# Windowed attention and a channel mix on one core: two phases over DRAM become one loop of 12 units kept on chip

## The chip, the cores and the metric

The kernel runs on one core of a Trainium2 chip. The metric is the time of one execution on the device in microseconds (us), taken as the median of several runs. One execution was also recorded by the hardware profiler; what is read from the profile and the trace is that execution. TensorE (PE) multiplies matrices, with its weight loads shown as PEld, VectorE is DVE, ScalarE is ACT, GpSimd is POOL, and SyncE (SP) issues DMAs.

## The reference

Inputs q, k, v are float32 of 4 batches x 8 heads x 768 tokens x 64. Each query sees the first 4 keys (the sinks) and the last 128 keys up to its own. The heads, side by side, are the 512 channels of x, which goes through a channel mix with a hidden width of 1024.

```python
scores = scale * np.matmul(q, k.transpose(0, 1, 3, 2))
keep = is_sink | in_window            # pos < 4, or 0 <= rel < 128
a = softmax(where(keep, scores, -1e9))
x = np.matmul(a, v)                   # heads side by side: (4, 768, 512)
x_prev = x shifted by one token, zero in front
xk = mu_k * x + (1.0 - mu_k) * x_prev
xr = mu_r * x + (1.0 - mu_r) * x_prev
k = np.maximum(xk @ w_k, 0.0)
v = k * k @ w_v
r = 1.0 / (1.0 + np.exp(-(xr @ w_r)))
out = r * v
```

## The kernel before

The kernel has two phases. The framework lists the instructions of each engine in an order of its own, made when the kernel is built, with the order of the source as priority; on the chip every engine follows its list, and waits where an input or a buffer is not ready.

The first phase loops over 4 batches x 8 heads. POOL issues three DMAs that load q, k and v of one head and turn them into bf16 (lines 90, 92 and 94). PE transposes q and k, 12 blocks of 128 tokens (lines 102 and 104), DVE copies them out of PSUM (106, 107). Then, for each of six tiles of 128 queries, PE makes the scores of one, two or three key blocks with a contraction of 64 (119), ACT takes the exponential (123), DVE multiplies with a mask (126), PE multiplies with v, which has a column of ones for the sum (130), and DVE takes the reciprocal and scales (134, 135). From the third tile on, the third key block is the first 128 keys, of which the mask keeps the 4 sinks. SP writes the head's result into `x_mid` in DRAM (137).

The second phase loops over the 4 batches. `prep` reads a batch of x back, transposes it (182), copies it (186), and makes xk and xr on DVE (190, 191, 194). `mm` makes the hidden layer in pieces of 384 tokens (206, with relu on ACT in 210 and the square on DVE in 211), then for each 128 tokens the value (219), the gate (223, sigmoid in 226), their product (228) and the DMA of the result. `prep` of the next batch is traced ahead of `mm` of this one. The weights are loaded once, by POOL (145, 147, 149).

## Time and profile before

| | |
|---|---|
| median of 3 runs | 352.32 us (352.17 to 352.41) |
| span of the profiled execution | 349.4 us, so some 2.9 us of a run lie around the span |
| PE busy | 295.4 us (85%) |
| DVE busy | 217.4 us (62%) |
| ACT busy | 139.9 us (40%) |
| POOL busy | 88.8 us (25%), nearly all of it issuing DMAs |

The profiled execution has no time of its own beside its span. The span goes from the first to the last instruction. Busy is the sum of what instructions take; matmuls overlap in the pipeline, so PE's time is better read from the distance between the starts of neighbouring matmuls. In a row of the timeline a run of n equal matmuls has its start and its whole length, so the distance is the length less that of one, divided by n - 1.

### The profile page before, as it was taken

What the parts mean: (1) busy time and instruction counts of PE and PEld (TensorE: products, weight loads), DVE (VectorE), ACT (ScalarE), POOL (GpSimd) and SP (SyncE); (2) the same over time, 40 slices, a digit from 0 to 9 for tenths busy, and PEclk for the clock granted to TensorE, in tenths of its full rate; (3) what the DMA queues carried; (4) which work ended last, traced back from release to release, by engine and by line L of the source; (5) the groups of instructions that cost most, each with busy time, mean ns of one, the idle gap of its engine ahead of it and who ended that gap; (6) DMA issues with size and microseconds to landing.
All of it is one profiled execution on the core that took longest, in us unless ns stands there. A gap on an engine that the chain in (4) does not pass through costs nothing.

```text
span 349.4 us, 5795 instructions
## 1 busy us (share of the span) xinstructions
PE 295.4 (85%) x1974; PEld 170.3 (49%) x1984; DVE 217.4 (62%) x778; ACT 139.9 (40%) x298; POOL 88.8 (25%) x166
## 2 busy tenths in 40 slices
PE   1678779879879879879889889688999999899994
PEld 1445445545545545545545546444545444445541
DVE  1555765865865765765765766899955329644422
ACT  1324333433433433433443445366517326534521
POOL 9626334244334234244244221000000000000000
PEclk9999999999999999999999999999999999999999
DMA  6999698798697797797896862130030030022022
GB/s 41 161 174 146 55 69 57 64 152 58 56 69 56 64 154 53 61 69 50 65 160 48 67 47 23 19 96 0 2 150 33 30 120 33 0 89 94 0 90 90
DMA packets 110125, 25.02 MB, mean 72 GB/s; under 512 B 101904, under 2 KB 106512, under 8 KB 110096
## 3 DMA queue, kind: packets, MB, share of 16 engines
q0 software_dynamic: 77360, 12.06, 47.5%
q1 hardware_dynamic: 32736, 12.59, 14.5%
q8 instruction: 15, 0.25, 0.3%
q14 instruction: 14, 0.11, 0.1%
HBM read 27.27 MB, written 9.44 MB: 105 GB/s over the span
## 4 chain that ended last, share of the span: by engine, by line
PE 72%; DVE 15%; DMA 4%; ACT 3%; issue 3%; POOL 2%; POOLq 0%; ACTq 0%
PE sps L119 19%; PE vps L219 12%; PE kps L206 11%; PE ops L130 11%; PE kT_ps L104 8%; PE qT_ps L102 7%; DMA qk_bf<-in_q_dram 4%; PE rps L223 4%; DVE e_sb L126 3%; DVE rec L134 3%; DVE xk_bf L191 2%; DVE xr_bf L194 2%; ACT e_sb L123 2%; DVE qkTsb L106 2%; PE xT_ps L182 1%
## 5 line engine op out<-in xcount | busy, mean ns | idle before, releaser
L123 ACT ACTIVATE e_sb<-sps 128x384 bf16<-128x384 f32 (+1 forms) x192 | 81.1, 437 | 136.1 <-PE sps L119 70.7
L119 PE MATMUL sps<-qkTsb 64*128 64x128 bf16 x480 | 83.0, 298 | 6.4 <-ACT e_sb L123 5.5
L130 PE MATMUL ops<-v_bf,e_sb 128*128 128x65 bf16 x480 | 56.0, 243 | 19.0 <-DVE e_sb L126 18.7
L134 DVE RECIPROCAL rec<-ops 128x1 f32<-128x1 f32 x192 | 31.5, 165 | 63.5 <-PE ops L130 59.2
L126 DVE TENSOR_TENSOR e_sb<-e_sb,mask 128x384 bf16<-128x384 bf16 (+1 forms) x192 | 59.2, 309 | 1.4
L130 PEld LDWEIGHTS <-e_sb 128*128 128x128 bf16 x480 | 31.4, 119 | 49.9 <-DVE e_sb L126 31.8
L119 PEld LDWEIGHTS <-qkTsb 64*128 64x128 bf16 x480 | 39.9, 118 | 29.1 <-issue 16.2
L135 DVE TENSOR_SCALAR res<-ops,rec 128x64 bf16<-128x64 f32 x192 | 50.0, 275 | 0.0
L206 PE MATMUL kps<-xk_bf,wk_sb 128*128 128x384 bf16 x256 | 47.6, 329 | 1.2 <-ACT ktmp L210 0.5
L219 PE MATMUL vps<-wv_sb,kk_bf 128*128 128x512 bf16 x185 | 43.7, 379 | 3.8 <-DVE kk_bf L211 3.5
L102 PE MATMUL qT_ps<-ident,qk_bf 128*64 128x128 bf16 x192 | 32.5, 309 | 15.4 <-DMA qk_bf<-in_q_dram 10.5
L90 POOL DMA_DIRECT2D qk_bf<-in_q_dram x32 | 26.4, 825 | 49.5 <-PE kT_ps L104 29.9
L104 PE MATMUL kT_ps<-ident,qk_bf 128*64 128x128 bf16 x192 | 38.0, 314 | 0.7 <-DMA qk_bf<-in_k_dram 0.7
L228 DVE TENSOR_TENSOR o_sb<-r_sb,vps 128x512 f32<-128x512 f32 x24 | 16.4, 687 | 34.6 <-ACT r_sb L226 28.4
L210 ACT ACTIVATE ktmp<-kps 128x384 bf16<-128x384 f32 x64 | 30.7, 491 | 16.4 <-PE kps L206 11.6
L206 PEld LDWEIGHTS <-wk_sb 128*128 128x128 bf16 x256 | 24.7, 98 | 21.5 <-issue 6.4
L94 POOL DMA_DIRECT2D v_bf<-in_v_dram x32 | 26.2, 820 | 33.7 <-PE sps L119 17.3
L102 PEld LDWEIGHTS <-qk_bf 128*64 128x64 bf16 x192 | 22.4, 160 | 19.3 <-DMA qk_bf<-in_q_dram 11.2
L219 PEld LDWEIGHTS <-kk_bf 128*128 128x128 bf16 x192 | 18.5, 98 | 26.1 <-DVE kk_bf L211 5.0
L226 ACT ACTIVATE r_sb<-rps 128x512 f32<-128x512 f32 x24 | 14.3, 598 | 42.3 <-PE rps L223 37.9
L211 DVE TENSOR_TENSOR kk_bf<-ktmp 128x384 bf16<-128x384 bf16 x64 | 22.3, 357 | 14.2 <-ACT ktmp L210 14.2
L104 PEld LDWEIGHTS <-qk_bf 128*64 128x64 bf16 x192 | 20.8, 151 | 12.7 <-issue 9.0
(39 smaller groups left out, 184.3 us busy)
## 6 DMA issues: line engine op xcount, KB each, us to landing
out_dram<-o_sb SPq DMA_DIRECT2D x24, 256.0 KB, 2.0
qk_bf<-in_q_dram POOLq DMA_DIRECT2D x32, 96.0 KB, 3.2
qk_bf<-in_k_dram POOLq DMA_DIRECT2D x32, 96.0 KB, 3.4
v_bf<-in_v_dram POOLq DMA_DIRECT2D x32, 96.0 KB, 3.4
x_mid<-res SPq DMA_DIRECT2D x32, 96.0 KB, 2.3
x_sb<-x_mid SPq DMA_DIRECT2D x4, 768.0 KB, 4.9
wk_sb<-in_moe_w_k_dram POOLq DMA_DIRECT2D x1, 1024.0 KB, 8.5
wv_sb<-in_moe_w_v_dram POOLq DMA_DIRECT2D x1, 1024.0 KB, 10.5
```

The costliest lines, as they stand in the source:

```text
L90: nc.gpsimd.dma_start(out=qk_bf[:, :, 0:D], in_=q[b, h].rearrange("(n p) d -> p n d", p=128))
L102: nc.tensor.transpose(out=qT_ps[:, 128 * t:128 * t + 128], in_=qk_bf[:, t, 0:D], identity=ident)
L104: nc.tensor.transpose(out=kT_ps[:, 128 * t:128 * t + 128], in_=qk_bf[:, t, D:2 * D], identity=ident)
L119: nc.tensor.matmul(out=sps[:, 128 * j:128 * j + 128], lhsT=kT[:, 128 * kj:128 * kj + 128], rhs=qs, start=True, stop=True)
L123: nc.scalar.activation(out=e_sb[:, 0:W], in_=sps[:, 0:W], func=AF.Exp, scale=scale)
L126: nc.vector.tensor_tensor(out=e_sb[:, 0:W], in0=e_sb[:, 0:W], in1=msk[:, 0:W], op=ALU.mult)
L130: nc.tensor.matmul(out=ops, lhsT=e_sb[:, 128 * j:128 * j + 128], rhs=v_bf[:, kj, :], start=(j == 0), stop=(j == nblk - 1))
L134: nc.vector.reciprocal(out=rec, in_=ops[:, D:D + 1])
L135: nc.vector.tensor_scalar(out=res[:, t, :], in0=ops[:, 0:D], scalar1=rec, scalar2=None, op0=ALU.mult)
L206: nc.tensor.matmul(out=ps, lhsT=wk_sb[:, c, 128 * f:128 * f + 128], rhs=xk_bf[:, c, SEQ_CHUNK * sc:SEQ_CHUNK * (sc + 1)], start=(c == 0), ...
L210: nc.scalar.activation(out=tmp, in_=ps, func=AF.Relu)
L219: nc.tensor.matmul(out=vps, lhsT=kk_bf[:, f, s0:s0 + 128], rhs=wv_sb[:, f, :], start=(f == 0), stop=(f == NF - 1))
```

## The change

The two phases become one loop over 12 units of 256 tokens, each with all 8 heads, and x never leaves the chip.

- SP loads q, k and v as float32, two units ahead; POOL turns them into bf16. Two heads lie side by side in the 128 partitions (a pair), so PE transposes full blocks, 16 for a unit.
- `attend` goes through the four pairs. The scores of a pair are six matmuls, whose operands are partitions 0 to 63 and 64 to 127 in turn. One exponential and one mask multiply cover both heads and 256 queries, 1024 columns. The sinks of all heads are one block-diagonal matrix: four matmuls give their scores for a unit, one exponential of 256 columns follows, and in the value product one matmul for each 128 queries adds them for both heads. One reciprocal and one multiply close a pair. Units that begin a batch have their sinks inside the first key block.
- `mix` transposes x in SBUF, and makes the difference of neighbouring tokens on POOL and xk and xr on DVE. `ffn` makes the hidden layer with pieces of 256 tokens, and the gate by a tanh, with half of w_v.
- The order of the source takes one pair of `attend`, one piece of `prepare` for the next unit, and one piece of `ffn` for the unit before, in turn.

```diff
-    x_mid = nc.dram_tensor("x_mid", (B, S, Dm), BF16, kind="Internal").ap()
...
-    for b in range(B):
-        for h in range(H):
...
-    def prep(b):
...
-    def mm(b, xk_bf, xr_bf):
...
+    const = ctx.enter_context(tc.tile_pool(name="const", bufs=1))
+    ld = ctx.enter_context(tc.tile_pool(name="ld", bufs=3))
+    kt_pool = ctx.enter_context(tc.tile_pool(name="kt", bufs=2))
+    qt_pool = ctx.enter_context(tc.tile_pool(name="qt", bufs=2))
+    e_pool = ctx.enter_context(tc.tile_pool(name="e", bufs=3))
+    es_pool = ctx.enter_context(tc.tile_pool(name="es", bufs=2))
+    x_pool = ctx.enter_context(tc.tile_pool(name="x", bufs=2))
+    kk_pool = ctx.enter_context(tc.tile_pool(name="kk", bufs=2))
+    r_pool = ctx.enter_context(tc.tile_pool(name="r", bufs=3))
+    sc_ps = ctx.enter_context(tc.tile_pool(name="sc_ps", bufs=2, space=PSUM))
+    tr_ps = ctx.enter_context(tc.tile_pool(name="tr_ps", bufs=1, space=PSUM))
+    o_ps = ctx.enter_context(tc.tile_pool(name="o_ps", bufs=1, space=PSUM))
+    mm_ps = ctx.enter_context(tc.tile_pool(name="mm_ps", bufs=2, space=PSUM))
...
+    def load(u):
+        b, T = divmod(u, NT)
+        qs = ld.tile([128, H, 128], FP32, name="qs")
+        ks = ld.tile([128, H, 128], FP32, name="ks")
+        parts = 2 if u == 0 else 1
+        n = H // parts
+        for i in range(parts):
+            hs = slice(i * n, (i + 1) * n)
+            for dst, src in ((ks, k), (qs, q)):
+                nc.sync.dma_start(
+                    out=dst[:, hs, :],
+                    in_=src[b, hs, 256 * T:256 * T + 256, :].rearrange(
+                        "h (p j) d -> p h (j d)", j=2))
+        vs = ld.tile([128, 2, H, D], FP32, name="vs")
+        for kb in range(2):
+            for j in range(2):
+                s0 = 256 * T + 128 * kb
+                nc.sync.dma_start(
+                    out=vs[64 * j:64 * j + 64, kb, :, :],
+                    in_=v[b, :, s0:s0 + 128, :].rearrange(
+                        "h (p j) d -> j p h d", j=2)[j])
+        qk_raw[u] = (qs, ks)
+        v_raw[u] = vs
+    load(0)
...
+    def fill_mask(m, blocks, sinks):
+        nc.gpsimd.memset(m, 1.0)
...
+    mask0 = const.tile([128, 2, 384], BF16, name="mask0")
+    fill_mask(mask0[:, 0, :], [(0, "D"), (128, "U"), (256, "D")], [(0, 256)])
+    nc.gpsimd.tensor_copy(out=mask0[:, 1, :], in_=mask0[:, 0, :])
...
+    v_bufs = [const.tile([128, 2, H, D + 1], BF16, name=f"v{i}") for i in range(3)]
+    for t in v_bufs:
+        nc.gpsimd.memset(t[:, :, :, D:D + 1], 1.0)
+    ksink = [const.tile([128, NP, 128], BF16, name=f"ksink{i}") for i in range(2)]
+    vsink = [const.tile([128, H, D + 1], BF16, name=f"vsink{i}") for i in range(2)]
+    for t in ksink + vsink:
+        nc.gpsimd.memset(t, 0.0)
...
+    load(1)
+    for h in range(H):
+        nc.gpsimd.dma_start(out=vs4[4 * h:4 * h + 4, :, 0:D],
+                            in_=v[:, h, 0:NS, :].rearrange("b s d -> s b d"))
...
+    def load_weights(after):
+        with tc.issue_after(after.ins):
+            nc.gpsimd.dma_start(out=wk_sb, in_=moe_w_k.rearrange("(c p) f -> p c f", p=128))
+            nc.gpsimd.dma_start(out=wr_sb, in_=moe_w_r.rearrange("(c p) f -> p c f", p=128))
+            nc.gpsimd.dma_start(out=wv_sb, in_=moe_w_v.rearrange("(c p) f -> p c f", p=128))
         for f in range(NF):
+            nc.vector.tensor_scalar(out=wv_h[:, f, :], in0=wv_sb[:, f, :], scalar1=0.5,
+                                    scalar2=None, op0=ALU.mult)
...
+    def prepare(u):
...
+        kb16 = qt_pool.tile([128, NP, 2, 2, D], BF16, name="kb16")
+        qb16 = qt_pool.tile([128, NP, 2, 2, D], BF16, name="qb16")
+        parts = 2 if u == 0 else 1
+        n = NP // parts
+        for i in range(parts):
+            cs = slice(i * n, (i + 1) * n)
+            for dst, src in ((kb16, ks), (qb16, qs)):
+                for j in range(2):
+                    last = nc.gpsimd.tensor_copy(
+                        out=dst[:, cs, j, :, :],
+                        in_=src[:, 2 * n * i:2 * n * (i + 1), 64 * j:64 * j + 64].rearrange(
+                            "p (c a) d -> p c a d", a=2))
+        for kb in range(2):
+            last = nc.gpsimd.tensor_copy(out=vb[:, kb, :, 0:D], in_=vs[:, kb, :, :])
+        marks[u] = last
+        kt = kt_pool.tile([128, 2, NP, 128], BF16, name="kt")
+        qt = qt_pool.tile([128, NP, 256], BF16, name="qt")
+        kps = tr_ps.tile([128, 2, NP, 2, 64], BF16, name="tps")
+        for c in range(NP):
+            for j in range(2):
+                nc.tensor.transpose(out=kps[:, :, c, j, :],
+                                    in_=kb16[:, c, j, :, :].rearrange("p a d -> p (a d)"),
+                                    identity=ident)
+        nc.vector.tensor_copy(out=kt, in_=kps.rearrange("p a c j t -> p a c (j t)"))
+        yield
+        qps = tr_ps.tile([128, NP, 2, 128], BF16, name="tps")
...
+        nc.scalar.copy(out=qt.rearrange("p c (t j) -> p c j t", j=2), in_=qps)
...
+        if T == 0:
...
+                    nc.gpsimd.tensor_copy(out=dst, in_=src)
+            nc.gpsimd.tensor_tensor(
+                out=vsink[b % 2][0:32, :, :], op=ALU.mult, in0=hmask,
+                in1=vs4[:, b:b + 1, :].to_broadcast([32, H, D + 1]))
+        yield
+    def attend(u, x):
...
+        if T > 0:
+            sps = tr_ps.tile([128, 256], FP32, name="tps")
+            for c in range(NP):
+                nc.tensor.matmul(out=sps, lhsT=ksink[b % 2][:, c, :], rhs=qt[:, c, :],
+                                 start=(c == 0), stop=(c == NP - 1))
+            es = es_pool.tile([128, 256], BF16, name="es")
+            nc.scalar.activation(out=es, in_=sps, func=AF.Exp, scale=scale)
+        lo = 0 if T > 0 else 128
+        for c in range(NP):
+            sc = sc_ps.tile([128, 2, 512], FP32, name="sc")
+            jobs = []
+            if T > 0:
+                jobs.append((kp[:, 1, c, :], 0, 128, 0))
+            jobs.append((kt[:, 0, c, :], 128, 384, 0))
+            jobs.append((kt[:, 1, c, :], 384, 512, 128))
+            for (lhs, o0, o1, q0) in jobs:
+                for a in range(2):
+                    rows = slice(64 * a, 64 * a + 64)
+                    nc.tensor.matmul(out=sc[:, a, o0:o1], lhsT=lhs[rows],
+                                     rhs=qt[rows, c, q0:q0 + o1 - o0],
+                                     start=True, stop=True)
+            e = e_pool.tile([128, 2, 512], BF16, name="e")
+            nc.scalar.activation(out=e[:, :, lo:], in_=sc[:, :, lo:], func=AF.Exp, scale=scale)
+            nc.vector.tensor_tensor(out=e[:, :, lo:], in0=e[:, :, lo:],
+                                    in1=(mask if T > 0 else mask0), op=ALU.mult)
+            o = o_ps.tile([128, 2, 2, D + 1], FP32, name="o")
+            for g in range(2):
+                if T > 0:
+                    nc.tensor.matmul(out=o[:, g, :, :], lhsT=es[:, 128 * g:128 * g + 128],
+                                     rhs=vsink[b % 2][:, 2 * c:2 * c + 2, :],
+                                     start=True, stop=False, skip_group_check=True)
+                for a in range(2):
+                    h = 2 * c + a
+                    steps = []
+                    if g == 0 and T > 0:
+                        steps.append((0, vp[:, 1, h, :]))
+                    if g == 1:
+                        steps.append((256, vb[:, 0, h, :]))
+                    steps.append((256 * g + 128, vb[:, g, h, :]))
+                    for i, (e0, rhs) in enumerate(steps):
+                        nc.tensor.matmul(out=o[:, g, a, :], lhsT=e[:, a, e0:e0 + 128], rhs=rhs,
+                                         start=(T == 0 and i == 0),
+                                         stop=(i == len(steps) - 1), skip_group_check=True)
+            rec = r_pool.tile([128, 2, 2, 1], FP32, name="rec")
+            nc.vector.reciprocal(out=rec, in_=o[:, :, :, D:D + 1])
+            nc.vector.tensor_tensor(
+                out=x[:, :, 128 * c:128 * c + 128].rearrange("p g (a d) -> p g a d", a=2),
+                in0=o[:, :, :, 0:D], in1=rec.to_broadcast([128, 2, 2, D]), op=ALU.mult)
+            yield
...
+    def mix(u, x):
...
+        xps = tr_ps.tile([128, NC, 256], BF16, name="tps")
+        for g in range(2):
...
+                nc.tensor.transpose(out=xps[:, c, 128 * g:128 * g + 128],
+                                    in_=x[:, g, 128 * c:128 * c + 128], identity=ident)
...
+        nc.vector.tensor_copy(out=xc[:, :, 2:258], in_=xps)
...
+        nc.gpsimd.tensor_tensor(out=td, in0=xc[:, :, 2:258], in1=xc[:, :, 1:257],
+                                op=ALU.subtract)
+        xk = x_pool.tile([128, NC, 256], BF16, name="xk")
+        xr = x_pool.tile([128, NC, 256], BF16, name="xr")
+        for dst, mu in ((xk, mu_k_sb), (xr, mu_r_sb)):
+            for c in range(NC):
+                nc.vector.scalar_tensor_tensor(
+                    out=dst[:, c, :], in0=td[:, c, :], scalar=mu[:, c:c + 1],
+                    in1=xc[:, c, 1:257], op0=ALU.mult, op1=ALU.add)
...
+    def ffn(u, xk, xr):
...
+        kk = kk_pool.tile([128, NF, 256], BF16, name="kk")
+        for f2 in range(NF // 2):
+            ps = mm_ps.tile([128, 2, 256], FP32, name="mm")
...
+                    nc.tensor.matmul(out=ps[:, i, :], lhsT=wk_sb[:, c, 128 * f:128 * f + 128],
+                                     rhs=xk[:, c, :], start=(c == 0), stop=(c == NC - 1),
+                                     skip_group_check=True)
+            rl = kk_pool.tile([128, 2, 256], BF16, name="rl")
+            nc.scalar.activation(out=rl, in_=ps, func=AF.Relu)
+            nc.vector.tensor_tensor(out=kk[:, 2 * f2:2 * f2 + 2, :], in0=rl, in1=rl,
+                                    op=ALU.mult)
+            if f2 % 2:
+                yield
+        for g in range(2):
+            tok = slice(128 * g, 128 * g + 128)
+            rps = mm_ps.tile([128, Dm], FP32, name="mm")
+            for c in range(NC):
+                nc.tensor.matmul(out=rps, lhsT=xr[:, c, tok], rhs=wr_sb[:, c, :],
+                                 start=(c == 0), stop=(c == NC - 1))
+            th = r_pool.tile([128, Dm], FP32, name="th")
+            nc.scalar.activation(out=th, in_=rps, func=AF.Tanh, scale=0.5)
+            vps = mm_ps.tile([128, Dm], FP32, name="mm")
             for f in range(NF):
+                nc.tensor.matmul(out=vps, lhsT=kk[:, f, tok], rhs=wv_h[:, f, :],
+                                 start=(f == 0), stop=(f == NF - 1))
+            o_sb = r_pool.tile([128, Dm], FP32, name="o_sb")
+            nc.vector.scalar_tensor_tensor(out=o_sb, in0=th, scalar=1.0, in1=vps,
+                                           op0=ALU.add, op1=ALU.mult)
+            s0 = 256 * T + 128 * g
             nc.sync.dma_start(out=out[b, s0:s0 + 128, :], in_=o_sb)
+            yield
+    drain(prepare(0))
+    load_weights(marks[0])
+    pend = None
+    for u in range(U):
+        if u + 2 < U:
+            load(u + 2)
+        x = x_pool.tile([128, 2, Dm], BF16, name="x")
+        filler = ffn(u - 1, *pend) if pend else iter(())
+        main = attend(u, x)
+        nxt = prepare(u + 1) if u + 1 < U else iter(())
+        for i, _ in enumerate(main):
+            if i >= 1:
+                next(nxt, None)
+            next(filler, None)
+        drain(filler)
+        drain(nxt)
+        pend = mix(u, x)
+    drain(ffn(U - 1, *pend))
```

## Rows read from the trace of the kernel before

**Rows 1.** Busy time by engine, and the clock in 40 slices, whole span.
```profile
PE 295.4 (85%) x1974; PEld 170.3 (49%) x1984; DVE 217.4 (62%) x778; ACT 139.9 (40%) x298; POOL 88.8 (25%) x166
...
PEclk9999999999999999999999999999999999999999
```
**Rows 2.** The chain of work that ended last, share of the span by engine.
```profile
PE 72%; DVE 15%; DMA 4%; ACT 3%; issue 3%; POOL 2%; POOLq 0%; ACTq 0%
```
**Rows 3.** Busy time in stretches: us, then us busy (instructions) by engine, clock, DMA.
```profile
20.00:212.00 192.00, 161.72 (x1218) 99.38 (x1218) 129.17 (x582) 72.95 (x173) 73.75 (x119) 1.00 0.90 80
...
250.00:280.00 30.00, 29.82 (x152) 14.69 (x152) 15.66 (x33) 11.83 (x24) 0.20 (x2) 1.00 0.17 67
```
**Rows 4.** Timeline of PE: start, us, instructions; one round of two heads.
```profile
104.65 0.80 PE L102 MATMUL qT_ps<-ident,qk_bf 128*64 128x128 bf16 x6 [0.30 <-DVE qkTsb L106]
...
106.80 0.31 PE L104 MATMUL kT_ps<-ident,qk_bf 128*64 128x128 bf16 x1
107.05 0.50 PE L119 MATMUL sps<-qkTsb 64*128 64x128 bf16 x3
107.48 0.24 PE L130 MATMUL ops<-v_bf,e_sb 128*128 128x65 bf16 x1
...
115.31 0.51 PE L130 MATMUL ops<-v_bf,e_sb 128*128 128x65 bf16 x6
...
117.85 0.37 PE L102 MATMUL qT_ps<-ident,qk_bf 128*64 128x128 bf16 x2 [0.30 <-DVE qkTsb L106]
```
**Rows 5.** Timeline of PE: matmuls of full height, second phase.
```profile
230.70 0.50 PE L182 MATMUL xT_ps<-ident,x_sb 128*128 128x128 bf16 x6
...
249.72 1.46 PE L206 MATMUL kps<-xk_bf,wk_sb 128*128 128x384 bf16 x8
...
253.66 7.07 PE L219 MATMUL vps<-wv_sb,kk_bf 128*128 128x512 bf16 x31
```
**Rows 6.** Groups by line and shape, DVE and ACT: xcount | busy us, mean ns | idle.
```profile
L123 ACT ACTIVATE e_sb<-sps 128x384 bf16<-128x384 f32 x128 | 62.6, 491 | 77.4 <-PE ops L130 53.6 <-PE sps L119 20.9 <-DVE e_sb L126 1.2
...
L126 DVE TENSOR_TENSOR e_sb<-e_sb,mask 128x384 bf16<-128x384 bf16 x128 | 43.3, 340 | 0.0
...
L134 DVE RECIPROCAL rec<-ops 128x1 f32<-128x1 f32 x192 | 31.5, 165 | 63.5 <-PE ops L130 59.2
...
L106 DVE COPY qkTsb<-qT_ps 64x768 bf16<-64x768 bf16 x32 | 17.4, 545 | 8.3 <-PE qT_ps L102 8.3
...
L228 DVE TENSOR_TENSOR o_sb<-r_sb,vps 128x512 f32<-128x512 f32 x24 | 16.4, 687 | 34.6 <-ACT r_sb L226 28.4 <-PE vps L219 5.4 <-issue 0.7
L191 DVE SCALAR_TENSOR_TENSOR xk_bf<-tdiff,mu_k_sb,xc 128x768 bf16<-128x768 bf16 x16 | 16.2, 1012 | 0.0
...
L226 ACT ACTIVATE r_sb<-rps 128x512 f32<-128x512 f32 x24 | 14.3, 598 | 42.3 <-PE rps L223 37.9 <-DVE o_sb L228 4.3
L186 ACT COPY xc<-xT_ps 128x768 bf16<-128x768 bf16 x16 | 12.7, 805 | 10.0 <-DVE xr_bf L194 7.5 <-PE xT_ps L182 2.5
...
L123 ACT ACTIVATE e_sb<-sps 128x128 bf16<-128x128 f32 x32 | 8.8, 275 | 49.8 <-PE sps L119 49.8
...
L126 DVE TENSOR_TENSOR e_sb<-e_sb,mask 128x128 bf16<-128x128 bf16 x32 | 6.9, 215 | 0.0
```
**Rows 7.** The same view, POOL.
```profile
L94 POOL DMA_DIRECT2D v_bf<-in_v_dram x32 | 26.2, 820 | 33.7 <-PE sps L119 17.3 <-PE ops L130 11.2 <-POOL v_bf L96 5.2
...
L63 POOL MEMSET mask<- 128x384 bf16 x1 | 0.4, 408 | 0.0
...
L64 POOL TENSOR_SCALAR_AFFINE_SELECT mask<-mask 128x128 bf16<-128x128 bf16 x1 | 0.3, 304 | 0.0
...
L49 POOL MEMSET mask<- 128x128 bf16 x1 | 0.2, 204 | 0.0
```
**Rows 8.** DMA queues (packets, MB, share of 16 engines) and issues (us to landing).
```profile
q1 hardware_dynamic: 32736, 12.59, 14.5%
...
out_dram<-o_sb SPq DMA_DIRECT2D x24, 256.0 KB, 2.0
...
v_bf<-in_v_dram POOLq DMA_DIRECT2D x32, 96.0 KB, 3.4
...
wk_sb<-in_moe_w_k_dram POOLq DMA_DIRECT2D x1, 1024.0 KB, 8.5
wv_sb<-in_moe_w_v_dram POOLq DMA_DIRECT2D x1, 1024.0 KB, 10.5
wr_sb<-in_moe_w_r_dram POOLq DMA_DIRECT2D x1, 512.0 KB, 7.0
```

More of the change, by code (lines that the diff above doesn't have):

```diff
@@ L13, with drain, interleave @@
 ALU = mybir.AluOpType
+PSUM = bass.MemoryType.PSUM
+def drain(gen):
+    for _ in gen:
+        pass
+def interleave(main, filler):
+    for _ in main:
+        next(filler, None)
+    drain(filler)
 @with_exitstack
@@ L167 @@
+    NS = 4
+    NT = S // 256
+    NP = H // 2
     NC = Dm // 128
     NF = Dff // 128
[L169 to L198 removed]
@@ L231 @@
-    pk = prep(0)
-    for b in range(B):
-        nk = prep(b + 1) if b + 1 < B else None
-        mm(b, *pk)
-        pk = nk
+    U = B * NT
+    scale = 1.0 / (D ** 0.5)
+    const = ctx.enter_context(tc.tile_pool(name="const", bufs=1))
[4 more added lines that the diff above has]
+    es_pool = ctx.enter_context(tc.tile_pool(name="es", bufs=2))
@@ new lines @@
+    load(0)
+    ident = const.tile([128, 128], BF16, name="ident")
+    make_identity(nc, ident)
+    def fill_mask(m, blocks, sinks):
+        nc.gpsimd.memset(m, 1.0)
+        for (lo, kind) in blocks:
+            for j in range(2):
+                sl = m[64 * j:64 * j + 64, lo:lo + 128]
+                if kind == "U":
+                    nc.gpsimd.affine_select(out=sl, in_=sl, compare_op=ALU.is_ge, fill=0.0,
+                                            base=j - 1, pattern=[[-1, 128]],
+                                            channel_multiplier=2)
+                else:
+                    nc.gpsimd.affine_select(out=sl, in_=sl, compare_op=ALU.is_ge, fill=0.0,
+                                            base=-j, pattern=[[1, 128]],
+                                            channel_multiplier=-2)
+        for (lo, hi) in sinks:
+            for j in range(2):
+                nc.gpsimd.memset(m[64 * j:64 * j + 2, lo:hi], 1.0)
@@ new lines @@
+    for t in v_bufs:
[4 more added lines that the diff above has]
+        nc.gpsimd.memset(t, 0.0)
+    hmask = const.tile([32, H, D + 1], BF16, name="hmask")
+    nc.gpsimd.memset(hmask, 1.0)
+    nc.gpsimd.affine_select(out=hmask, in_=hmask, compare_op=ALU.is_ge, fill=0.0, base=0,
+                            pattern=[[-4, H], [0, D + 1]], channel_multiplier=1)
```

228 lines of the change are left out of this document (64 added, 164 removed).

## Prediction

> **What bounds the kernel now.** I read the busy times first: PE is busy for 85% of the span, no other engine for more than 62%, and the granted clock is at its upper level, 2.4 GHz, in all 40 slices [rows 1]. The chain of waits says the same: 72% of it is PE, 15% DVE [rows 2]. The stretches then show two different phases [rows 3]. In the mix phase 30 us hold PE for 29.8 us. In the attention phase PE is busy for 161.7 of 192 us, DVE for 129.2.
>
> What PE's time is made of stands in its timeline. One round of two heads goes from 104.65 to 117.85, so 6.6 us a head [rows 4]. Three scores of a half-height operand take 0.50 us, which is 0.10 each after the first; six value matmuls take 0.51, 0.054 each; a transpose in six takes 0.107 to 0.11. Next to them stand the changes between half-height scores and full-height work: a transpose starts at 106.80 and the score behind it 0.25 later, the last score of 107.05 starts 0.20 in and the value matmul follows 0.23 behind it, at 107.48. So a change costs some 0.14 us beyond the usual distance. Between the two ends of that round eleven blocks of scores make 22 changes, 1.5 us a head. A head then asks of PE 15 x 0.10 + 15 x 0.054 + 12 x 0.107 + 1.5 = 5.1 of its 6.6 us: 78%. In the mix phase the distances are 0.163 us at 384 columns, 0.22 at 512, and 0.05 for a full-height transpose [rows 5]; a batch has 64, 72 and 24 of these, 27.5 us of its 30: 91%.
>
> **The change, part by part.** PE first, for a unit that does not begin a batch.
>
> - Transposes: 16 for q and k and 8 for x, at 0.05: 1.2 us. Before, q and k had 384 half-width ones at 0.107, 41 us in all; now 192 full ones, 10 us.
> - Scores: 24 matmuls, 4,096 columns. If the two halves still go one after the other, the columns pass at the 512-column rate of 0.42 ns: 0.43 us a pair. With weight loads showing as in the rows it is 4 x 0.107 + 2 x 0.16 = 0.75. If the halves run side by side it is 0.22. I take 0.5, near the middle row, 2.0 a unit.
> - Changes of height: two a pair, entered mostly from 512-column matmuls; I take 0.3 a pair, 1.2 a unit (0 to 2).
> - Sink scores: four of 256 columns; between 0.05 at 128 and 0.163 at 384 I read 0.107. 0.4 us.
> - Values: 40 matmuls of 65 or 130 columns at 0.055: 2.2 us.
> - Mix: 32 x 0.107 + 24 x 0.22 = 8.7 us.
>
> That is 15.7 us. The four units that begin a batch have no sink work, 16 fewer value matmuls and a quarter fewer score columns: 13.9. Twelve units: 8 x 15.7 + 4 x 13.9 = 181 us. The same counting before gives 32 x 5.1 + 4 x 27.5 = 273. The change removes a third of PE's time: the 128-key block that was computed for 4 sinks, half the transposes, and most of the changes of height, which were 22 in each of 16 rounds.
>
> On the halves: partitions 64 to 127 hold no scores before, so no row shows them side by side. The Trainium skill, TensorEngine Tiling (Array Packing), Key Properties, says that different tiles of the array can load and multiply in parallel. By that the scores would cost 0.22 a pair and the sum fall by 13 us.
>
> DVE, from the slopes and fixed parts of its groups [rows 6]: a mask multiply is 0.15 + 0.49 ns a column, so 0.65 for 1,024, four make 2.6; reciprocals 4 x 0.165; the closing multiply of 256 columns out of PSUM lies below the 0.69 of 512, at 0.43, four make 1.7; two copies of 1,024 at 0.7; eight multiply-adds of 256 columns at 1.01 - 512 x 1.04 ns = 0.48, 3.8; four squares of 512 at 0.40; two products at 0.69. Sum 13.2 us a unit, 150 or so in all. ACT: four exponentials of 1,024 at 0.17 + 0.84 ns a column = 1.03, one of 256, one copy of 1,024 at 1.0, four relus and two tanhs of 512 at 0.6: 9.1 us. Both fit beside PE's 15.7.
>
> POOL changes its trade: its 96 input DMAs go, six conversions of 512 columns and one difference of 1,024 come. Nothing like them is in the trace. From below a memset's 0.1 + 0.8 ns a column [rows 7] gives 0.5 and 0.9; from above the 0.30 of an affine select of 128 columns, all of it scaled, gives 1.2 and 2.4, twice that for two inputs. I take 0.75 and 2.3 (nearest to the select less its fixed part): 7 us a unit, hidden under PE; the two-unit head start covers the loads. Each unit moves 4,096 load packets and 256 out; at the 25 ns a packet of the hardware queue (14.5% of 16 x 349.4 us over 32,736) that is 7 us of the 16 engines, hidden too [rows 8]. The bounce through `x_mid` costs little now and gives little.
>
> What is not hidden. **The start:** POOL first makes masks, zeroed tiles and head masks: by its rows some 10 us of memsets, selects and copies, and eight small DMAs at 0.82, so 17 us; eight conversions for unit 0, 2.4; transposes, copy, transposes, copy, 3. The first score comes at 22.4 us. **Unit 0** has no mix beside it: one pair takes score 0.4, exponential 0.8, mask 0.55, values 0.6, closing 0.6 and gaps, 3.5; the others follow at the distance of the single `o` buffer, 1.6: 8.3 us. **Weights** are queued behind the conversions, at about 21 us; landing took 8.5, 7.0 and 10.5 us [rows 8], one behind the other until 47. The value of unit 0 waits for the last, and PE has about 15 us of other work from 31 on: 3 us. **The end:** the last x is transposed, copied (0.7), differenced (2.3) and mixed (1.9) before the last mix starts: 5.3; then product 0.7, its DMA 2.0 and a little: 3.1.
>
> The sum: 181 less unit 0's 5 is 176 us of PE work from 31 us on. Attention work ran at 78% and mix work at 91%; by their shares of 77 and 104 us that is 85%, and 176 / 0.85 = 207. So 22.4 + 8.3 + 207 + 3 + 8.4 = 249 us of span, and with the 2.9 around it 252. I give 254, for the shorter queue of one transpose bank (`tr_ps`, used four times a unit) and two `kt` buffers, which let the next unit's keys out of PSUM only after the last score of this one.
>
> **Rivals.**
>
> *The halves overlap and the mix fills every gap.* PE at 168 us and 90%: 22 + 8 + 163 / 0.9 + 3 + 8 + 3 = 225. For it: mix work is always at hand, and it ran at 91%. Against: the attention's order was also free before, and got 78%.
>
> *POOL and DVE take turns.* Masks, squares and multiply-adds read two inputs from SBUF, 8 us a unit; POOL's 7 us read SBUF as well. If neither runs beside the other, DVE and POOL together take 13.2 + 7 = 20.2 us a unit, more than PE. 11.5 units of that, 232, with 42 us of start, unit 0, end and surroundings: 275; with POOL at its upper price (7.2 + 4.8 = 12), 332. The trace can't tell: POOL did little but DMA issues, 0.82 us each, with DVE busy for two thirds of the time. The Trainium skill, SBUF — State Buffer, its section on the two separate sides, speaks for this rival: it says that VectorE with two SBUF inputs and a GpSimd instruction that reads SBUF hold one port pair exclusively, the later blocked until the earlier ends.
>
> *Slower than before: the pairs run one after another.* Its place is PE's fixed order. If the value matmuls of a pair stand right behind its scores, PE waits each time for exponential and mask, and the closing multiply for the next `o`: 0.5 + 1.03 + 0.65 + 0.85 + 0.6 + 0.7 of gaps = 4.4 us a pair, 48 pairs 211. With the mix beside none of it, 104 / 0.91 = 114, and start and end 34: 359. It is slower if less than 7 us of the mix falls into those waits. Against it: before, scores of later tiles do go ahead of values [rows 4], and two `sc` buffers allow it here.
>
> **Chances.** The forecast (239 to 268) 0.56; tight 0.18 (215 to 239); turns 0.21 (268 to 332); one after another 0.04; no change 0.01. A difference under 0.2% can't be told from none. Faster 0.95, same 0.01, slower 0.04. The range of 8 in 10 runs from 226, which leaves out half of the tight case, to 294, which leaves out a quarter of the turns.
>
> **What would show it.** PE busy densely from some 35 us to the end, units about 18 us apart; scores starting 0.1 us apart or in pairs; the first score near 22 us; the weights landed by 47; DVE near 150 us, ACT near 107, POOL near 100. Wrong would be a DVE or POOL that is never idle in the units, conversions above 1.2 us, PE waiting for masks at every pair, or units above 20 us.

## The result and the profile after

The changed kernel takes 260.23 us (median of 4 runs, 259.94 to 262.93); the kernel before took 352.37 beside it. The ratio is 0.7399, with an interval of 0.7365 to 0.7433. Forecast were 254 us and a range of 226 to 294. The profiled execution has a span of 258.8 us. Medians are over all runs of a kernel; where these spread by more than 1.5%, the ratio rests on the faster ones alone.

First the page: busy times, and the slices of PE, of its clock and of the DMA engines, 6.5 us each ([rows 1] before).

```profile
PE 185.0 (72%) x1664; PEld 117.5 (45%) x1664; DVE 168.2 (65%) x344; ACT 103.8 (40%) x141; POOL 103.7 (40%) x181
...
PE   0015510589889599699796796997969979889493
...
PEclk9999999999979979899999799999999979979889
DMA  7999999400694681754967403011020110201102
```

PE's busy time fell by 110 us, but so did its density: 72% of the span instead of 85%. Two things show. Slices 6 and 7 of PE are nearly empty (1 and 0), and the row of PE's clock, flat before, now dips in places. The chain by engine and by line ([rows 2] before):

```profile
PE 52%; DVE 22%; DMA 10%; POOL 7%; ACT 5%; issue 2%; POOLq 1%; DVEq 0%; ACTq 0%
```

PE holds 52% of the chain instead of 72%; the shares of DVE, DMA and POOL have grown. The stretches (busy time of PE, PEld, DVE, ACT and POOL, clock, DMA share, GB/s; before, [rows 3]) are the standstill, the first unit behind it, a stretch of the steady loop, and the end:

```profile
32.00:48.00 16.00, 1.02 (x8) 0.44 (x7) 2.23 (x10) 0.57 (x1) 3.19 (x6) 1.00 1.14 209
48.00:67.80 19.80, 18.59 (x141) 11.47 (x142) 15.25 (x27) 8.93 (x12) 10.09 (x12) 1.00 0.06 18
150.00:170.00 20.00, 17.38 (x172) 10.92 (x169) 16.10 (x37) 9.29 (x14) 6.34 (x7) 1.00 0.10 34
240.00:258.80 18.80, 11.25 (x65) 6.59 (x63) 7.62 (x16) 3.58 (x6) 1.89 (x1) 0.88 0.11 43
```

**The standstill.** The timeline of all engines behind the gap, then the issues of the weights (KB, us to landing; [rows 8] before):

```profile
45.72 1.71 DVE L174 TENSOR_SCALAR wv_h<-wv_sb 128x512 bf16<-128x512 bf16 x8 [15.55 <-DMA wv_sb<-in_moe_w_v_dram]
47.34 0.18 DVE L289 RECIPROCAL rec<-o 128x4 f32<-128x4 f32 x1
47.56 0.42 DVE L290 TENSOR_TENSOR x<-o,rec 128x256 bf16<-128x256 f32 x1
...
48.04 0.71 PE L304 MATMUL tps<-ident,x 128*128 128x128 bf16 x5 [14.40 <-DVE x L290]
```
```profile
wk_sb<-in_moe_w_k_dram POOLq DMA_DIRECT2D x1, 1024.0 KB, 9.9
wv_sb<-in_moe_w_v_dram POOLq DMA_DIRECT2D x1, 1024.0 KB, 19.4
...
wr_sb<-in_moe_w_r_dram POOLq DMA_DIRECT2D x1, 512.0 KB, 12.6
```

The last weight landed near 46 us, close to the forecast 47. But the program halves it on DVE (`wv_h`), and in DVE's list these eight instructions stand ahead of a reciprocal and a closing multiply of unit 0. DVE waits 15.55 us for a weight, and x, which needs no weight, comes late by that: PE waits 14.40.

**The joint of two units.** DVE and POOL beside each other at one joint, and PE behind it:

```profile
65.83 0.69 DVE L268 TENSOR_TENSOR e<-e,mask 128x1024 bf16<-128x1024 bf16 x1 [0.46 <-ACT e L267]
...
68.63 0.68 DVE L311 COPY xc<-tps 128x1024 bf16<-128x1024 bf16 x1
69.79 2.11 DVE L268 TENSOR_TENSOR e<-e,mask 128x1024 bf16<-128x1024 bf16 x1 [0.47 <-ACT e L267]
71.82 1.66 DVE L320 SCALAR_TENSOR_TENSOR xk<-td,mu_k_sb,xc 128x256 bf16<-128x256 bf16 x4
```
```profile
69.46 1.89 POOL L314 TENSOR_TENSOR td<-xc 128x1024 bf16<-128x1024 bf16 x1 [1.37 <-DVE xc L311]
```
```profile
70.72 0.32 PE L263 MATMUL sc<-qt,kt 64*128 64x128 bf16 x3 [0.43 <-ACT e L267]
72.35 0.27 PE L333 MATMUL mm<-xk,wk_sb 128*128 128x256 bf16 x1 [1.31 <-DVE xk L320]
...
72.81 3.01 PE L333 MATMUL mm<-xk,wk_sb 128*128 128x256 bf16 x15
```

The difference `td` runs on POOL from 69.46 to 71.35. A mask multiply begins on DVE at 69.79 and ends at 71.90; in an undisturbed place it takes 0.69, as at 65.83. Then xk can start, 0.47 us after `td` is done, and PE has waited 1.31 us. At 73.6, among the fifteen matmuls of the hidden layer (line 333, hidden matmuls from here on), the granted clock falls to its lower level, 1.2 GHz. There are seven such stretches of 3.41 us, each beginning in a wait of PE of 1.3 to 3.6 us or within 1.6 us behind it, and one in the last 0.9 us: 24.8 us of the span, which agrees with its mean granted clock of 0.952 (258.8 x 0.048 x 2). A wait isn't followed by a fall each time: three waits of 1.3 us, with the first hidden matmul at 125.9, 160.7 and 177.7, are not.

At two of the three joints that go over to a new batch, PE waits for a mask instead:

```profile
87.43 3.52 DVE L268 TENSOR_TENSOR e<-e,mask 128x768 bf16<-128x768 bf16 x1 [0.22 <-ACT e L267]
```

Such a mask takes 0.56 us undisturbed. Beside it POOL runs a product for the sinks, `td` and two conversions one behind the other, until 90.53; the mask ends at 90.95, and PE has waited 2.86 us for it.

The groups of DVE's masks and POOL's work (busy us, mean ns), and who waited:

```profile
L268 DVE TENSOR_TENSOR e<-e,mask 128x1024 bf16<-128x1024 bf16 x32 | 35.6, 1112 | 8.2 <-ACT e L267 8.2
...
L314 POOL TENSOR_TENSOR td<-xc 128x1024 bf16<-128x1024 bf16 x12 | 22.7, 1890 | 69.1 <-DVE xc L311 69.1
...
L202 POOL CAST v<-vs 128x512 bf16<-128x512 f32 x24 | 14.2, 625 | 32.0 <-PE o L285 32.0
```
```profile
PE mm L333 <- DVE xk L320: 13.4, 11, 3.6
```

**The rate of the matmuls.** The row of the clock shows 9 for the first eleven slices, but the distances of the matmuls tell otherwise. Ten and fifteen hidden matmuls of the changed kernel, and six transposes of the kernel before:

```profile
55.24 2.29 PE L333 MATMUL mm<-xk,wk_sb 128*128 128x256 bf16 x10 [0.43 <-DVE xk L320]
...
126.40 1.97 PE L333 MATMUL mm<-xk,wk_sb 128*128 128x256 bf16 x15
...
146.24 2.29 PE L333 MATMUL mm<-xk,wk_sb 128*128 128x256 bf16 x10 [0.16 <-DVE xk L320]
```
```profile
228.81 0.85 PE L182 MATMUL xT_ps<-ident,x_sb 128*128 128x128 bf16 x6
```

At 146.24 the granted clock is at 1.2 GHz, and ten take 2.29 us, 0.21 apart; at 126.40, at 2.4 GHz, fifteen take 1.97, most of them 0.109 apart. The ten at 55.24 take 2.29 as well. The trace's record of the clock begins only at 59.9 us; up to there the distances are those of the lower level. In the kernel before, the record begins at 230.4 us: six transposes take 0.85 at 228.81, 0.107 apart, and the same six take 0.50 at 230.70 [rows 5], 0.056 apart. Its whole attention phase has these distances, 0.107 for transposes and 0.054 for value matmuls [rows 4], the rate of the lower level; the flat row of 9 in [rows 1] does not show that. In the changed kernel PE had been busy for 10.7 of the 11.9 us from 48.0 on when the rate rose.

**PE's small matmuls** ([rows 4] before): two pairs of scores, and values early, behind long matmuls, and after a long wait.

```profile
24.10 0.51 PE L285 MATMUL o<-v,e 128*128 128x65 bf16 x6 [0.17 <-DVE e L268]
...
66.77 0.28 PE L285 MATMUL o<-v,e 128*128 128x65 bf16 x4
...
68.30 0.62 PE L263 MATMUL sc<-qt,kt 64*128 64x128 bf16 x12
...
143.71 0.36 PE L285 MATMUL o<-v,e 128*128 128x65 bf16 x6 [2.85 <-DVE e L268]
```

Twelve scores, two pairs, start within 0.40 us (0.62 less the last one's 0.22), 0.2 a pair: matmuls of the two halves start 4 ns apart. Value matmuls stand 0.03 apart at the upper level ((0.28 - 0.19) / 3), after a wait of 2.85 us too, where six take 0.36. Six at 24.10, before the rate rose, take 0.51, as the row of before [rows 4] and so its 0.054.

### The profile page after: what moved, and what is told of

Same layout as the page of the kernel before. It is cut to its first block, busy times and chain, and to the rows that moved or that the text cites. A ratio compares the mean times of both kernels' runs of the same rounds, so it can differ in the third digit from the quotient of the medians.

```text
span 258.8 us, 4357 instructions
## 1 busy us (share of the span) xinstructions
PE 185.0 (72%) x1664; PEld 117.5 (45%) x1664; DVE 168.2 (65%) x344; ACT 103.8 (40%) x141; POOL 103.7 (40%) x181
## 4 chain that ended last, share of the span: by engine, by line
PE 52%; DVE 22%; DMA 10%; POOL 7%; ACT 5%; issue 2%; POOLq 1%; DVEq 0%; ACTq 0%
PE mm L352 16%; PE mm L333 16%; DVE e L268 11%; PE mm L346 8%; DMA wv_sb<-in_moe_w_v_dram 7%; DVE xk L320 5%; PE o L285 5%; ACT e L267 4%; DMA vs<-in_v_dram 2%; PE sc L263 2%; DVE xr L320 2%; PE tps L217 2%; PE o L273 2%; PE tps L304 1%; POOL vs L154 1%
## 5 line engine op out<-in xcount | busy, mean ns | idle before, releaser
L333 PE MATMUL mm<-xk,wk_sb 128*128 128x256 bf16 x384 | 62.5, 313 | 13.5 <-DVE xk L320 13.4
L267 ACT ACTIVATE e<-sc 128x1024 bf16<-128x1024 f32 (+1 forms) x48 | 44.4, 954 | 57.5 <-PE sc L263 50.3
L268 DVE TENSOR_TENSOR e<-e,mask 128x1024 bf16<-128x1024 bf16 (+1 forms) x48 | 52.0, 1083 | 13.0 <-ACT e L267 13.0
L337 ACT ACTIVATE rl<-mm 128x512 bf16<-128x512 f32 x48 | 28.4, 597 | 55.5 <-PE mm L333 53.1
L314 POOL TENSOR_TENSOR td<-xc 128x1024 bf16<-128x1024 bf16 x12 | 22.7, 1890 | 69.1 <-DVE xc L311 69.1
L352 PE MATMUL mm<-wv_h,kk 128*128 128x512 bf16 x192 | 47.5, 379 | 0.0
L285 PE MATMUL o<-v,e 128*128 128x65 bf16 x352 | 22.5, 202 | 11.5 <-DVE e L268 9.9
L285 PEld LDWEIGHTS <-e 128*128 128x128 bf16 x352 | 17.7, 103 | 22.4 <-DVE e L268 18.0
L338 DVE TENSOR_TENSOR kk<-rl 128x512 bf16<-128x512 bf16 x48 | 21.5, 447 | 7.4 <-ACT rl L337 7.3
L220 ACT COPY qt<-tps 128x1024 bf16<-128x1024 bf16 x12 | 15.7, 1309 | 23.6 <-PE tps L217 23.4
L346 PE MATMUL mm<-wr_sb,xr 128*128 128x512 bf16 x96 | 25.1, 379 | 0.0
L320 DVE SCALAR_TENSOR_TENSOR xk<-td,mu_k_sb,xc 128x256 bf16<-128x256 bf16 x48 | 21.8, 513 | 2.1 <-POOL td L314 2.1
```

The lines of the kernel that those rows point to most:

```text
L267: nc.scalar.activation(out=e[:, :, lo:], in_=sc[:, :, lo:], func=AF.Exp, scale=scale)
L268: nc.vector.tensor_tensor(out=e[:, :, lo:], in0=e[:, :, lo:], in1=(mask if T > 0 else mask0), op=ALU.mult)
L285: nc.tensor.matmul(out=o[:, g, a, :], lhsT=e[:, a, e0:e0 + 128], rhs=rhs, start=(T == 0 and i == 0), stop=(i == len(steps) - 1), skip_grou ...
L314: nc.gpsimd.tensor_tensor(out=td, in0=xc[:, :, 2:258], in1=xc[:, :, 1:257], op=ALU.subtract)
L320: nc.vector.scalar_tensor_tensor(out=dst[:, c, :], in0=td[:, c, :], scalar=mu[:, c:c + 1], in1=xc[:, c, 1:257], op0=ALU.mult, op1=ALU.add)
L333: nc.tensor.matmul(out=ps[:, i, :], lhsT=wk_sb[:, c, 128 * f:128 * f + 128], rhs=xk[:, c, :], start=(c == 0), stop=(c == NC - 1), skip_gro ...
```

## The experiments

**Halving moved into the relu.** Undoes the halving on DVE alone.

```diff
-        for f in range(NF):
-            nc.vector.tensor_scalar(out=wv_h[:, f, :], in0=wv_sb[:, f, :], scalar1=0.5,
-                                    scalar2=None, op0=ALU.mult)
...
-    nc.scalar.activation(out=rl, in_=ps, func=AF.Relu)
+    nc.scalar.activation(out=rl, in_=ps, func=AF.Relu, scale=0.5 ** 0.5)
...
-                nc.tensor.matmul(out=vps, lhsT=kk[:, f, tok], rhs=wv_h[:, f, :],
+                nc.tensor.matmul(out=vps, lhsT=kk[:, f, tok], rhs=wv_sb[:, f, :],
```

> The halving of w_v on DVE is left out; the same factor goes into the relu's scale (its square is 0.5). Theory 'order of DVE': DVE, PE and ACT stand still from 34 to 48 us only because the eight halving multiplies, which wait for the last weight, stand in DVE's list ahead of the closing multiply of unit 0. Then that gap shrinks to 2 or 3 us and the kernel takes 245 to 250 us. Rival 'arrival': work of units 0 and 1 would run out anyway until the last weight lands at 45.7 us; then the gap only moves to the first value matmul of the mix, and the time stays within 4 us of 260.

Measured: 249.66 us (246.17 to 250.28), ratio 0.7019 [0.6957, 0.7082]. The standstill is gone; the matmuls that use this weight (line 348, unit 0's channel mix) wait for it only at their own place (PE's weight loads):

```profile
47.02 0.11 PEld L348 LDWEIGHTS <-kk 128*128 128x128 bf16 x2 [0.35 <-DMA wv_sb<-in_moe_w_v_dram]
```

So it was the order on DVE, not the landing itself.

**`td` on VectorE.** One word: `nc.gpsimd` becomes `nc.vector` in line 314.

> The difference of neighbouring tokens (1.89 us, 12 times) goes from POOL to DVE, where it should take 0.7. Theory 'turns are covered': DVE's blocked time lies beside PE work, what counts is the wait of PE for xk at each unit, 1.6 us in eleven units, which gets some 1.2 us shorter; 245 to 252 us, and the mask multiplies fall from a mean of 1.11 to 0.8 or 0.9 us. Rival 'turns bound': DVE and POOL together set the pace; then each unit gains the whole 1.9 less 0.7 and the shorter blocks besides, over 2 us in each of 12 units, 235 us or less. Third: DVE is the bound; then 8 us more on it, 265.

Measured: 242.04 us (240.68 to 243.06), 0.6859 [0.6822, 0.6895]; 18 us off, between the two ranges that were expected. Units follow at 15.6 us on average where it was 17.2. The tile, the masks, the wait for xk:

```profile
L314 DVE TENSOR_TENSOR td<-xc x12: 696/698/810, 48.7 to 223.7; 128x1024 bf16<-128x1024 bf16 x12
```
```profile
L268 DVE TENSOR_TENSOR e<-e,mask 128x1024 bf16<-128x1024 bf16 x32 | 25.3, 790 | 4.3 <-ACT e L267 4.3
```
```profile
PE mm L333 <- DVE xk L320: 3.6, 4, 2.3
```

DVE has more to do and is quicker through it. The time at the lower clock falls from 24.8 to 10.2 us. Two explanations stayed open: 1.9 us of `td` in front of xk, or DVE held up by POOL.

**`td` on both.** The kernel with `td` on VectorE; POOL makes it again for nobody.

```diff
+        td2 = x_pool.tile([128, NC, 256], BF16, name="td2")
+        nc.gpsimd.tensor_tensor(out=td2, in0=xc[:, :, 2:258], in1=xc[:, :, 1:257],
+                                op=ALU.subtract)
```

> The kernel with td on VectorE (242.0), and in it GpSimd forms the same difference once more, into a tile that nobody reads: the second subtraction is work added, the output stays. Theory A: what td on GpSimd cost was that VectorE's masks and interpolations stand still while GpSimd runs its two-input operation; then the idle copy of it costs most of the 18 us again: 252 to 260, with masks at 1.0 us or more as before. Theory B: it was only that td itself took 1.9 us in front of xk; an operation that nobody waits for is then free: 240 to 245.

Measured: 272.7 us (272.19 to 274.09), 0.7738 [0.7682, 0.7794]: an operation whose result nobody reads costs 30.7 us. DVE's timeline at one joint, POOL's there, and DVE's `td` in all:

```profile
106.47 2.42 DVE L314 TENSOR_TENSOR td<-xc 128x1024 bf16<-128x1024 bf16 x1
```
```profile
106.45 1.89 POOL L317 TENSOR_TENSOR td<-xc 128x1024 bf16<-128x1024 bf16 x1 [3.41 <-DVE xc L311]
```
```profile
L314 DVE TENSOR_TENSOR td<-xc x12: 696/1558/3760, 48.8 to 253.6; 128x1024 bf16<-128x1024 bf16 x12
```

DVE's subtraction, 0.70 alone, begins with POOL's and takes 2.42, about POOL's 1.89 and its own time one after the other. In six of the twelve joints DVE begins first; then its own takes 0.70, POOL's 2.40, and a mask behind it 2.38. So a blocked engine alone is enough for a loss, and the latency alone, by which the added operation would be free, is refuted as the whole account. How the 18 us of the changed kernel divide between the two isn't shown: at its joint above, `td` itself ends only 0.47 us before xk starts. The loss is larger than either theory had it: both subtractions now start on the same xc, and from the end of xc to the start of xk one joint takes 3.0 us (69.05 to 72.08), where it took 2.5 in the changed kernel (69.31 to 71.82) and 1.3 with `td` on VectorE alone (68.00 to 69.32). PE waits 17.2 us for xk, and 41.8 us run at the lower clock.

**Conversions of q and k on ScalarE.**

```diff
-                    last = nc.gpsimd.tensor_copy(
+                    last = nc.scalar.copy(
```

> The conversions of q and k, four of the six of a unit, go from POOL to ACT, which then has 11 to 12 us a unit. The mask multiplies and multiply-adds of DVE meet POOL less often. Theory 'turns cost where PE waits': the difference of tokens stays on POOL, so PE's wait for xk stays; masks fall from a mean of 1.11 to some 0.95 us, and the time to 252 to 259 us. Rival 'turns bound': 2.8 us a unit come off the sum of POOL and DVE, 225 to 235 us. Third: exponentials wait behind conversions in ACT's list, 260 to 270.

Measured: 245.59 us (243.13 to 249.45), 0.6895 [0.6857, 0.6934]. Better than expected, and not for the reason asked about: from 104.1 to 223.4 the last seven units take 17.0 us each, as in the changed kernel, 121.3 to 240.0. So taking the conversions off POOL does not shorten the steady loop. They do hold masks up, 1.09 us beside a conversion instead of 0.69, and the mask of 3.52 us takes 2.47 here; whether that costs nothing, or ACT with its new work and the clock (31.3 us at the lower level) take it back, was not separated. The gain is the start: ACT has little to do there, and PE transposes keys at 4.88 and scores at 11.64, where the changed kernel's first score comes at 22.0.

```profile
4.42 0.71 ACT L197 CAST kb<-ks 128x256 bf16<-128x256 f32 x2 [1.22 <-DMA ks<-in_k_dram]
```
```profile
11.64 0.82 PE L263 MATMUL sc<-qt,kt 64*128 64x256 bf16 x8 [1.38 <-ACT qt L220]
```

**The scores in another order**, three matmuls of one half, then three of the other.

```diff
-            for (lhs, o0, o1, q0) in jobs:
-                for a in range(2):
+            for a in range(2):
+                for (lhs, o0, o1, q0) in jobs:
```

> The scores of a pair go through one half of the partitions first, then the other, in place of turn by turn. Theory 'halves side by side': in the changed kernel two matmuls of different halves start 3 to 6 ns apart, so a pair costs 0.2 us of PE; one half after the other brings 0.25 to 0.45 us back for each of 48 pairs, and PE is the bound for most of a unit: 5 to 15 us slower. Rival 'PE has slack': the scores wait for ACT and DVE anyway, then within 2 us of 260.

Measured: 267.06 us (266.58 to 268.33), 0.7576 [0.7535, 0.7617]. The size is as expected, but the trace doesn't carry the reason. Where two pairs are queued the halves still run side by side, 10 ns apart, and 12 scores still take 0.62 us:

```profile
68.05 0.62 PE L263 MATMUL sc<-qt,kt 64*128 64x128 bf16 x12
```

Over some 207 distances between neighbouring scores the mean rose by 6 ns, 1.2 us in all. PE's waits for xk grew (19.9 instead of 13.4 us), but those of the values for masks shrank by as much (3.4 instead of 9.9), and 34.1 us instead of 24.8 run at the lower clock. Where the other 5 us come from was not found.

**No taking turns:** all of `attend`, then `prepare`, then `ffn`, in the source.

```diff
-        for i, _ in enumerate(main):
-            if i >= 1:
-                next(nxt, None)
-            next(filler, None)
-        drain(filler)
+        drain(main)
         drain(nxt)
+        drain(filler)
```

> The order of the source no longer takes turns: all four pairs of attention, then the preparation of the next unit, then the whole mix of the unit before. Theory: the framework's own list already goes by what is ready, so it still lays mix matmuls into the waits of the pairs; 258 to 275 us. Rival 'one after another' of the prediction: without the turns PE stands waiting for mask and exponential at each pair, 4.4 us a pair and the mix beside none of it; over 320 us.

Measured: 269.33 us (267.28 to 269.77), 0.7623 [0.7581, 0.7665]; most units 18.4 us apart, 17.9 on average. The written order is worth 9 us, far from what pairs one after another would take.

**Three buffers for `kt` and `qt`** (`bufs=2` to `bufs=3`).

> A third buffer for the transposed keys (kt) and for the transposed and converted queries (qt, kb16, qb16). Theory: the prediction's 2 us for the shorter queue of two kt buffers; 256 to 259 us. Rival: the one transpose bank in PSUM, not kt, holds the next unit's keys back, or nothing does; 260 within 1.5 us.

Measured: 261.47 us (258.17 to 265.54), 0.7337 [0.7286, 0.7387]; no difference that this can tell.

**Both, halving and `td`.**

> Both: the halving of w_v by the relu's scale, and the difference of tokens on DVE. Theory: the two act in different stretches (34 to 48 us, and each unit's joint), so the gains add: 260.2 - 10.6 - 18.2 = 231 us, 229 to 234. Rival: what the start gains is spent on waiting for the last weight or the loads of units 2 and 3, which were far ahead only because of the standstill; 236 to 242.

Measured: 226.57 us (223.25 to 227.38), 0.6431 [0.6406, 0.6457]: 33.7 off, where the two alone give 10.6 and 18.2. It is quicker than the range of 229 to 234, but by the ratios and their intervals (13.4, 19.0 and 34.1 us, each within 3) that the two add to more isn't shown. The page of this version:

```profile
PE 177.0 (79%) x1664; PEld 111.4 (50%) x1664; DVE 157.0 (70%) x348; ACT 103.4 (46%) x141; POOL 80.0 (36%) x169
...
PE   0004565998997998998998989988989999899592
...
PEclk9999999799999999999997999999999999999999
```

**Weights earlier:** in that version, right behind unit 0's conversions, the small loads of `vs4` behind them.

```diff
+        if u == 0:
+            load_weights(last)
+            for h in range(H):
+                nc.gpsimd.dma_start(out=vs4[4 * h:4 * h + 4, :, 0:D],
+                                    in_=v[:, h, 0:NS, :].rearrange("b s d -> s b d"))
```

> As the run with both, and POOL issues the weights right behind the conversions of unit 0 and the eight small sink loads behind the weights. Theory: POOL's list sets the first score: the conversions no longer stand behind 6 us of small DMAs, so the first score comes at 16 in place of 22 us and the last weight lands at 38 to 42 us; 5 to 7 us faster than with both alone. Rival: the 16 DMA engines, full from 0 to 40 us, set it; the weights only push the loads of units 1 and 2 back, within 2 us of the run with both.

Measured: 238.75 us (237.62 to 239.76), 0.6757 [0.6724, 0.679], 12 us slower than without. Both theories missed a new wait, in POOL's timeline, and PE's behind it:

```profile
25.88 0.57 POOL L200 DMA_DIRECT2D vs<-in_v_dram  x1 [5.07 <-DMA wk_sb<-in_moe_w_k_dram]
...
35.96 0.57 POOL L200 DMA_DIRECT2D vs<-in_v_dram  x1 [6.21 <-DMA wv_sb<-in_moe_w_v_dram]
...
37.73 1.17 POOL L190 CAST kb<-ks 128x512 bf16<-128x512 f32 x2
```
```profile
38.40 0.29 PE L207 MATMUL tps<-ident,kb 128*128 128x128 bf16 x1 [14.21 <-POOL kb L190]
```

POOL's issues of 2 KB wait until weights have landed, and unit 1's conversions stand behind them.

**Unit 0's conversions on ScalarE**, in the version with both.

```diff
+                    conv = nc.scalar.copy if u == 0 else nc.gpsimd.tensor_copy
```

> The kernel with the halving moved and td on VectorE, and in it unit 0's conversions of q and k on ScalarE instead of GpSimd. Theory A: with the standstill gone, GpSimd's list of small DMA issues and conversions still sets the first score (22 us), and ScalarE brings it forward by 8 to 10 us, as it did where all conversions were on ScalarE; the later units keep their 15.8 us, so 226.6 falls to 216 to 222. Theory B: the landing of the last weight (near 46 us) sets when unit 0's mix can begin, so what is gained at the start is waited away before the value matmuls: within 2 us of 226.6.

Measured: 222.73 us (222.1 to 224.24), 0.6333 [0.631, 0.6357]: the quickest of all, 3.8 off, just above the range of theory A. The first score comes at 11.05, and most of the gain is waited away, not for a weight but for POOL's list: 3.31 us for unit 0's v, 4.04 for unit 1's k. x is transposed at 30.3 instead of 32.7.

```profile
17.45 0.32 PE L282 MATMUL o<-v,e 128*128 128x65 bf16 x3 [3.31 <-POOL v L199]
...
25.62 0.29 PE L206 MATMUL tps<-ident,kb 128*128 128x128 bf16 x1 [4.04 <-POOL kb L194]
```

**Without the sinks in eight units**, in the version with both.

> The kernel with the halving moved and td on VectorE, without the sink scores, their exponential and the sink value matmuls in the 8 units that do not begin a batch (so their outputs lack the sink terms; their value sums begin at the first block of keys). Theory A: TensorE sets the pace, and each of these 8 units is shorter by the sinks' TensorE time: 0.84 us a unit by the rows of before, 7 us in all, 219 to 221. Theory B: a chain of VectorE and ScalarE sets the pace, and TensorE's time goes into its waits: within 2 us of 226.6.

Measured: 226.12 us (224.38 to 228.69), 0.6399 [0.6363, 0.6434], no difference that this can tell, where the rows of before promised 7 us. That speaks against PE as what alone sets the pace of that version, but doesn't settle it: in the traced run, the longest of the four, nine units take 137.3 us (54.8 to 192.1) where they take 140.6 with the sinks (52.6 to 193.2), and the start and the end, with some 10 us more at the lower clock, take it back.

**PE's wait filled**, in the changed kernel.

```diff
+            for _ in range(5 if f2 == 0 and u > 0 else 0):
+                nc.tensor.matmul(out=ps, lhsT=ident, rhs=wk_sb[:, 0, 0:512],
+                                 start=True, stop=True, skip_group_check=True)
```

> The changed kernel (260.2) with five matmuls of 512 columns, added ahead of the first hidden matmul of each unit but the first, into the tile that this matmul overwrites: TensorE computes something unused while it would wait 1.3 to 1.6 us for xk. Theory A: the fall of the granted clock to 1.2 GHz behind these joints comes of TensorE standing idle there; filled, most of the 26.8 us at the lower level go, and as work takes twice as long at it, up to 13 us come off: 247 to 254. Theory B: the clock falls there for another reason, or the loop is paced by VectorE at these places: 258 to 264, and more if the added 1.1 us a unit does not fit into the wait.

Measured: 265.88 us (264.71 to 267.87), 0.7551 [0.7485, 0.7617]. Time at the lower clock falls from 24.8 us (the 26.8 of the expectation counts on beyond the end of the span) to 10.2, so the idle joint does go with the fall of the clock; but 5.7 us are lost. The filling did not stay in the wait: it went in front of the next scores.

```profile
103.45 0.82 PE L331 MATMUL mm<-wk_sb,ident 128*128 128x512 bf16 x2
104.18 0.60 PE L248 MATMUL tps<-qt,ksink 128*128 128x256 bf16 x4
104.62 0.59 PE L331 MATMUL mm<-wk_sb,ident 128*128 128x512 bf16 x2
```

What the clock alone costs stays open.

## Why the prediction was right, and where it was not

The direction and the size held: 260.2 against 254, 6.2 us apart. The parts held less well than the sum, and that it came so close is in part luck: prices that were too high and losses that were not foreseen nearly cancel.

**The start** was right: first score forecast at 22.4, measured at 22.0, by POOL's list.

**Weights: the term that was mis-sized.** "PE has about 15 us of other work from 31 on: 3 us." Landing was right, and most of the 15 us were there (PE is busy for 12.6 us from 31 to 47 with the halving gone, for 1.3 with it), but PE couldn't reach them: the halving stood on DVE ahead of the closing multiply that they needed. PE stood for 14.4 us, 11.4 more than forecast. The prediction counted what waits for a landing by its data and not what stands behind the waiting instruction on its engine. That alone is more than the whole difference: the other terms came to 258.8 - 14.4 = 244.4 us of span against the forecast 249 - 3 = 246; the rest is 2.9 forecast around the span against 1.7 here (260.5 less 258.8 in the profiled run), and the 2 us for `tr_ps` and `kt`, of which the run with three `kt` buffers shows nothing beyond the intervals (`tr_ps` was not tried).

**The loop** came out at 17.2 us a unit (67.8 to 240.0, ten units), forecast near 18, by two errors that cancel. PE's work was put too high: scores at 0.5 a pair where 0.2 were measured, values at 0.055 where 0.03 were. These prices rest on [rows 4], a stretch at the lower rate, while the loop runs mostly at the upper. A unit is then 15.7 - 4 x 0.3 - 40 x 0.025 = 13.5 us, and an estimated 13.2 on average over the ten, of which three begin a batch. And the 85% at which PE would get through it was too high: 13.2 / 17.2 is 77%. With `td` on VectorE it is 13.2 / 15.6 = 85%.

**The halves** run side by side, as the first rival had it: starts 4 ns apart. The Trainium skill, TensorEngine Tiling (Array Packing), Key Properties, says that different tiles of the array can load and multiply in parallel. The trace agrees. That rival's 225 us needed PE to be 90% full as well, which the changed kernel didn't have. The version without both faults takes 226.6, which does not confirm that rival: its value matmuls were priced at the lower rate too, and PE is busy for 79% of that span.

**POOL and DVE taking turns** is real, and was priced wrongly as a rival for the whole kernel. Masks took 1.11 instead of 0.65 us and DVE 168 us instead of 150. What costs is mainly one place, `td` beside the masks in front of xk; the conversions, six of the seven instructions that were forecast for POOL in a unit, hold masks up too, but taking four of them off POOL did not shorten the loop. The Trainium skill, SBUF — State Buffer, on the two separate sides, says that a VectorE instruction with two SBUF inputs and a GpSimd one that reads SBUF exclude each other until the earlier ends. The runs agree: 0.70 us became 2.42 beside 1.89. POOL's prices were 0.63 to 0.72 a conversion (forecast 0.75) and 1.89 for `td` (2.3), both in the bounds.

**Pairs one after another** did not happen; even without turns in the source it was 269, not 359.

**The clock** was taken as flat at 2.4 GHz, as [rows 1] had it. By the distances, the attention phase before ran at the rate of 1.2 GHz up to 230.4 us and the changed kernel up to 59.9. So the third of PE's time that the forecast saw removed, 273 us to 181, is in part rate: attention's 163 of the 273 was priced at the lower rate. With 163 halved that is an estimated 192 us, and 8 x 13.5 + 4 x 12.4 = 158 after: less by about a fifth. The half-width transposes, priced at twice the full ones, were not dearer for their width: full-width ones take 0.107 as well before 230.4. How much of the 92 us gained is less work and how much is rate no run separates. Later the clock fell again where PE had waited, for less time in the run with less waiting for xk, 24.8 to 10.2 us, and for more in the one with more, 41.8.

**The end:** from the last x transposes to the end 18.8 us, of which the forecast's mix takes 8.7, so 10.1 where 8.4 was forecast; the last stretch ran partly at the lower clock (0.88 on average).
